# Rounding weights by their bits: a clamp, a shift and an integer addition in place of exponent times factor

## The chip, the cores and the metric

The kernel runs on one core of one Trainium2 chip. The metric is the device time of one execution in microseconds (us); less is better. The core's engines are TensorE (PE, matrix products; PEld is its loading of stationary operands), VectorE (DVE), ScalarE (ACT), GpSimd (POOL) and SyncE (SP, which here only issues DMAs). Each engine works through its own queue in order and waits on semaphores for the others.

## The reference

Attention over 8 batches, 12 heads, 448 positions and 64 dimensions per head, with RMS normalisation of q and k, followed by a two-layer product with squared ReLU. All in numpy; the two weight matrices arrive in double precision (they are float32 random numbers times a numpy float64 scalar), which is why the kernel has to turn pairs of 32-bit words into float32.

```python
def rmsnorm(x, g):
    return x / np.sqrt(np.mean(x * x, axis=-1, keepdims=True) + 1e-06) * g
q_n, k_n = rmsnorm(q, g_q), rmsnorm(k, g_k)              # (8, 12, 448, 64)
scores = 1.0 / np.sqrt(64) * (q_n @ k_n.transpose(0, 1, 3, 2))
attn = softmax(scores)                                    # over the last axis
x = (attn @ v).transpose(0, 2, 1, 3).reshape(3584, 768)
h = x @ w_in                                              # w_in  (768, 2048), float64
g = np.maximum(h, 0.0) ** 2
out = g @ w_out                                           # w_out (2048, 768), float64
```

## The kernel before

`attention_then_ffn_bounded` is the path that runs with these inputs. It works on four spans of two batches each. For a span it does the attention of 12 pairs of heads, then a first product (x times w_in, ReLU, square) and a second product (times w_out). Both products are done by a Strassen-like scheme: each product of 2 x 2 blocks takes seven block products, for which each block of weights is needed as seven combinations (`A11, S2, S1, S3, A12, A22, S4`; `A21` serves only to make others). After the first span the products of one span run beside the attention of the next.

**The weights are rounded and combined once, during the first span**, and written to DRAM (`w1s`, `w2s`); from there `load_blocks` brings them back, block by block, into a ring of five `sw` tiles (the DMA at line 647) for every span. `load_blocks` goes no further than `written[0]` allows, the count of pieces that have been written.

There are 32 pieces of 128 x 768 weights (16 of each matrix). `load_w` loads piece n as pairs of 32-bit words (786 KB; lines 528 and 531) into one of six places: one in `gC`, two in `gT`, three tiles named `words`; the last piece, 31, takes place 3. `prepare(t)` is tick t of a software pipeline. It is a generator of four steps, and several pieces are in flight in it. Before the change, for piece n:

- tick n, step 1: DVE takes the exponent out of the high words (L579); step 3: ACT clamps it in two activations (L592, L593), the second giving the bits of a scale.
- tick n+1, step 2: DVE puts in the sign (L584); step 3: DVE takes the mantissa's bits (L596); step 4: DVE adds the low words times 2^-32 (L604).
- tick n+2, step 1: ACT turns that into the factor (L576); steps 3 and 4: POOL multiplies exponent part by factor, one half of 384 columns at a time, into the block (`value`, L560), and after odd pieces makes the combinations S1 and S2 (`total`, L566).
- tick n+3, step 3: S3 and S4 (L566).
- tick n+4, step 1: SP writes the seven blocks of two pieces to DRAM (L572, 1.376 MB).

`load_words` at the end of a tick loads ahead up to piece t+3, into places that are free. `weights(upto)` takes steps from the generator. Four are taken before the first scores. Then each of the 12 iterations of `attention_alone` takes four more (eight in the first), in the place of its first `yield`: behind the four score products and the exponentials, ahead of `values(i)` and `finish(i)`. So 52 steps, 13 ticks, go by in the attention; the rest is spread evenly over the first product's 56 units of work (a unit is three products of 128 x 128 by 448, and is followed by the unit's DVE and ACT work on the result):

```python
EARLY, ALL = 4 * 13, 4 * (2 * NFC + 4)
weights(min(EARLY, 8 + (EARLY - 8) * (u + 1) // (NAT - 1)))
weights(min(ALL, EARLY + (ALL - EARLY) * (u - 1) // (N1 - 6)))
```

From unit 6 of the first product on, two PSUM banks that the scores had used hold intermediate bits (`bits`, `mantissa`); before that, the intermediate results stay in SBUF.

Other names: in the attention `sc` are scores (L752), `pr` their exponentials (ACT, L757), `pav` the products with v (L807), `tot` the row sums (L810); `finish` divides: a reciprocal (L821) and a product (L824), which gives `pav`'s bank back. `combine_x` makes differences of x for the first product (L837 to L839). In the first product `pa` to `pd` are results in PSUM (L962), `p`, `z`, `y` partial sums (L966, L969, L972), `gT` the activations (L977, L935, L937). L666, L683, L315, L325 and L679 are loads of q, k and v.

Of the kernel before, what the change touches and what calls it, by code (L numbers as in the profile page):

```python
# [9 lines left out]
F32 = mybir.dt.float32  # L10
U32 = mybir.dt.uint32
AF = mybir.ActivationFunctionType
ALU = mybir.AluOpType
# [373 lines left out]
def attention_then_ffn_bounded(  # L387
# [35 lines left out]
    nc = tc.nc  # L423
# [4 lines left out]
    P = 128  # L428
# [3 lines left out]
    NFC = DFF // P  # L432
# [14 lines left out]
    consts = ctx.enter_context(tc.tile_pool(name="consts", bufs=1))  # L447
# [3 lines left out]
    ps_s = ctx.enter_context(tc.tile_pool(name="ps_s", bufs=2, space=bass.MemoryType.PSUM))  # L451
# [3 lines left out]
    qk, qkT, ident, mhalf, gains, rstd0, _ = held  # L455
# [4 lines left out]
    clamp1 = consts.tile([P, 1], F32, name="clamp1")  # L460
    clamp2 = consts.tile([P, 1], F32, name="clamp2")

# [2 lines left out]


    doubles = w_in.dtype != F32
    words_in = 2 if doubles else 1  # L470
    w1r, w2r = ((w.bitcast(U32) if doubles else w).rearrange("(c p) n -> p c n", p=P) for w in (w_in, w_out))
    stage = gC.rearrange("p i f n -> p (i f n)")
    NW = NPAIR * P
    HW = HC * P
    WORDS, BLOCKS, EXPS, LAST = 6, 2, 4, 31

    EARLY, ALL = 4 * 13, 4 * (2 * NFC + 4)
    assert DM == NW and BLOCKS * 8 * HW + EXPS * NW + 2 * NW <= 3 * HF * S and 2 * NW <= 4 * S and HF % 4 == 0


# [1 line left out]
    A11, S2, S1, S3, A12, A22, S4 = range(7)  # L482
    A21 = 7
# [3 lines left out]
    def pairs_of(words):  # L487
        both = words.rearrange("p (n two) -> p n two", two=2)
        return both[:, :, 0], both[:, :, 1]

    def place_of(n):

        return n % WORDS if n < LAST else 3

    def words_of(n):
        place = place_of(n)
        if place == 0:
            at = BLOCKS * 8 * HW + EXPS * NW
            flat = stage[:, at:at + 2 * NW]
        elif place < 3:  # L500
            f = (NFC, HF)[place - 1] - 2
            flat = gT[:, f:f + 2, :].rearrange("p f n -> p (f n)")[:, 0:2 * NW]
        else:
            if (n, "words") not in spare:
                spare[n, "words"] = spare["pool"].tile([P, 2 * NW], F32, tag="words", name="words", bufs=WORDS - 3)
            flat = spare[n, "words"]
        return flat.bitcast(U32)

    def blocks_of(n):
        at = n // 2 % BLOCKS * 8 * HW  # L510
# [8 lines left out]
    spare, banks, bits = {}, {}, {}  # L519

    def load_w(n):

        if n < 2 * NFC:
            f = n % NFC // 2 + n % 2 * HF
            dst = words_of(n)[:, 0:words_in * NW]
            dst = dst if doubles else dst.bitcast(F32)
            if n < NFC:
                nc.sync.dma_start(dst.rearrange("p (c m) -> p c m", c=NPAIR),
                                  w1r[:, :, words_in * f * P:words_in * (f + 1) * P])
            else:  # L530
                nc.sync.dma_start(dst, w2r[:, f])

    def load_words(t, done):

        while loaded[0] <= t + 3 and all(
                place_of(m) != place_of(loaded[0]) for m in range(max(done, 0), loaded[0])):
            load_w(loaded[0])
            loaded[0] += 1

    def prepare(t):  # L540

        def there(n):
            return 0 <= n < 2 * NFC

        def parts(n):
            low, high = pairs_of(words_of(n))
            return exponents_of(n), exponents_of(n).bitcast(U32), low, low.bitcast(F32), high

        def value(n, half):
            if not there(n):
                return

            to = ((A11, A12), (A21, A22)) if n < NFC else ((A11, A21), (A12, A22))
            dst = blocks_of(n)[:, to[n % 2][half]]
            part = slice(half * HW, (half + 1) * HW)
            if doubles:
                e, _, _, f, _ = parts(n)
                nc.gpsimd.tensor_tensor(dst, f[:, part], e[:, part], ALU.mult)  # L560
            else:
                nc.gpsimd.tensor_copy(dst, words_of(n).bitcast(F32)[:, part])

        def total(n, dst, x, y, op):
            if there(n) and n % 2:
                nc.gpsimd.tensor_tensor(*[blocks_of(n)[:, i] for i in (dst, x, y)], op)  # L566

        n = t - 4
        if there(n) and n % 2:
            c = n % NFC // 2  # L570
            dst = w1s[c] if n < NFC else w2s[:, c // 4, :, c % 4]
            nc.sync.dma_start(dst.rearrange("k p m -> p k m"), blocks_of(n)[:, 0:7])  # L572
            written[0] = n + 1
        if there(t - 2) and doubles:
            f = parts(t - 2)[3]
            nc.scalar.activation(f, f, AF.Copy, bias=1.0, scale=2.0 ** -20)  # L576
        if there(t) and doubles:
            e, eu, low, f, high = parts(t)
            nc.vector.tensor_scalar(eu, high, 20, 0x7FF, ALU.logical_shift_right, ALU.bitwise_and)  # L579
        yield  # L580
        if there(t - 1) and doubles:

            e, eu, low, f, high = parts(t - 1)
            nc.vector.scalar_tensor_tensor(eu, high, 0x80000000, bits.pop(t - 1), ALU.bitwise_and, ALU.bitwise_or)  # L584
        if t < 3:
            load_words(t, t - 2)
        yield
        if there(t) and doubles:

            e, eu, low, f, high = parts(t)  # L590
            bits[t] = banks.get("bits", eu)
            nc.scalar.activation(e, eu, AF.Relu, bias=clamp1, scale=-1.0)  # L592
            nc.scalar.activation(bits[t], e, AF.Relu, bias=clamp2, scale=-(2.0 ** 23))  # L593
        if there(t - 1) and doubles:
            mantissa = banks.get("mantissa", parts(t - 1)[4])
            nc.vector.tensor_scalar(mantissa, parts(t - 1)[4], 0xFFFFF, None, ALU.bitwise_and)  # L596
        total(t - 3, S3, A11, A21, ALU.subtract)
        total(t - 3, S4, A12, S2, ALU.subtract)
        value(t - 2, 0)
        yield  # L600
        if there(t - 1) and doubles:

            e, eu, low, f, high = parts(t - 1)
            nc.vector.scalar_tensor_tensor(f, low, 2.0 ** -32, mantissa, ALU.mult, ALU.add)  # L604
        value(t - 2, 1)
        total(t - 2, S1, A21, A22, ALU.add)
        total(t - 2, S2, S1, A11, ALU.subtract)
        load_words(t, t - 2)
        yield

    def ticks():
        for t in range(2 * NFC + 4):
            yield from prepare(t)

    preparing = ticks()
# [421 lines left out]


    load_v(0)
    nc.vector.memset(clamp1, 1151.0)  # L1040
    nc.vector.memset(clamp2, 255.0 * 2.0 ** 23)

    def ahead(u, nxt):

# [9 lines left out]
    with tc.tile_pool(name="words", bufs=2) as spare["pool"]:  # L1054
        for _ in range(2):
            load_w(loaded[0])
            loaded[0] += 1
        load(2)
        norm(1)
        with tc.tile_pool(name="first", bufs=2, reuse_waits="tile") as work:  # L1060
            places_for(work, NJ)
            sums["ones"] = work.tile([SP, D], F32, tag="ones", name="ones", bufs=1)
            nc.vector.memset(sums["ones"], 1.0)
            weights(4)
            for u, _ in enumerate(attention_alone()):


                weights(min(EARLY, 8 + (EARLY - 8) * (u + 1) // (NAT - 1)))
                if u == NAT - 2:
                    load_blocks(5)  # L1070
        with tc.tile_pool(name="first_product", bufs=2, reuse_waits="tile") as work:
            for u, _ in enumerate(first_product(work, 0)):
                if u == 6:

                    for name in ("bits", "mantissa"):
                        bank = ps_s.tile([P, 2, 512], F32, tag="s", name=name)
                        banks[name] = bank.rearrange("p a b -> p (a b)")[:, 0:NW].bitcast(U32)
                weights(min(ALL, EARLY + (ALL - EARLY) * (u - 1) // (N1 - 6)))
                if u == N1 - 5:
                    norm(NAT + 1)  # L1080
                if u == N1 - 4:
                    transposes(NAT)
                    squares(NAT + 2)
    for span in range(NSPAN):
# [7 lines left out]
        with tc.tile_pool(name="second_product", bufs=2, reuse_waits="tile") as work:  # L1092
            rest = second_product(work, span)
            if more:
# [3 lines left out]
                total, done = HC * (7 * HF + 4) - 20, 0  # L1098
# [95 lines left out]
```

## Time and profile before

| | |
|---|---|
| median of 6 runs | 1411.95 us (1411.6 to 1412.8) |
| profiled execution: time, span | 1412.06 us, 1410.3 us |
| mean granted TensorE clock | 0.997 |
| PE busy | 1389.4 us, 99% of the span |
| DVE, ACT, POOL busy | 818.1, 450.2, 576.8 us |
| HBM read, written | 154.54 MB, 33.16 MB |

The page gives, for each engine, its busy time in the whole span, and then in 40 equal slices in tenths; `PEclk` is the granted clock, `DMA` the mean busy share of the 16 DMA engines. The chain that ended last follows back from the last instruction to what released it, step by step; "issue" in it is time in which an engine waited for nothing that the profile shows. In the timeline, the brackets give the idle time ahead of an instruction and what ended it. Durations of matrix products overlap, since they are pipelined and two of the attention's products run side by side.

### The profile page before, as it was taken

To read this page: it belongs to the slowest core of one execution; us is meant where nothing else is said; L and a number is where in the kernel's file an instruction comes from. 1 tells how busy PE (TensorE), PEld (TensorE's weight loads), DVE (VectorE), ACT (ScalarE), POOL (GpSimd) and SP (SyncE) were. 2 spreads that over 40 slices of the span, in tenths; PEclk is the share of its full clock that TensorE was granted. 3 is DMA by queue.
4 is the path that set the end of the run, shared out by engine and by line. 5 is a ranking of instruction groups with operands and counts; after the bars stand their busy time and mean duration, and the time that the engine had idled before them with its cause. 6 is when DMAs were issued, how large, how long until landed. Compare 5 with 4: busy or idle time off the path is not lost.

```text
span 1410.3 us, 14598 instructions
## 1 busy us (share of the span) xinstructions
PE 1389.4 (99%) x4518; PEld 643.3 (46%) x4518; DVE 818.1 (58%) x1388; ACT 450.2 (32%) x652; POOL 576.8 (41%) x400
## 2 busy tenths in 40 slices
PE   7999999999999999999999999999999999999997
PEld 3343454444444455444444455444444445555553
DVE  6778787589976333567776623457777633332111
ACT  6887588532332011233233111223233201110000
POOL 5877688544443122545444112445434312221000
PEclk9999999999999999999999999999999999999999
DMA  8576799644665333344566333345555333324443
GB/s 241 166 219 179 264 378 337 203 106 106 137 124 124 100 86 87 103 112 106 126 131 120 91 104 90 91 106 121 118 117 113 94 100 86 90 84 108 107 108 72
DMA packets 430915, 188.79 MB, mean 134 GB/s; under 512 B 277484, under 2 KB 428780, under 8 KB 430828
## 3 DMA queue, kind: packets, MB, share of 16 engines
q1 hardware_dynamic: 421228, 179.05, 48.8%
q10 hardware_dynamic: 9472, 8.72, 2.3%
q8 instruction: 38, 0.62, 0.2%
q14 instruction: 49, 0.40, 0.1%
q0 software_dynamic: 128, 0.00, 0.0%
HBM read 154.54 MB, written 33.16 MB: 133 GB/s over the span
## 4 chain that ended last, share of the span: by engine, by line
PE 95%; DMA 1%; DVE 1%; ACT 1%; POOL 1%; issue 0%; DVEq 0%; ACTq 0%; POOLq 0%
PE ps L1010 36%; PE sc L752 12%; PE pav L807 11%; PE pd L962 10%; PE pc L962 10%; PE pa L962 9%; PE pb L962 5%; PE tot L810 3%; DMA sw<-w1s 1%; PE pt L738 1%; DMA words<-in_moe_w_out_dram 0%; POOL rstd L335 0%; DVE xT L821 0%; POOL gC L566 0%; DVE rstd L333 0%
## 5 line engine op out<-in xcount | busy, mean ns | idle before, releaser
L1010 PE MATMUL ps<-gT,sw 128*128 128x448 f32 x768 | 299.1, 542 | 0.0
L720 POOL TENSOR_TENSOR half<-half,mhalf 128x28 f32<-128x28 f32 x36 | 173.3, 4814 | 262.1 <-DVE half L719 224.2
L1010 PE MATMUL ps<-gC,sw 128*128 128x448 f32 x576 | 225.2, 542 | 0.0
L939 POOL TENSOR_TENSOR gT<-gT 128x448 f32<-128x448 f32 x96 | 93.6, 976 | 311.9 <-ACT gT L935 311.9
L1010 PEld LDWEIGHTS ps<-gT,sw 128*128 128x128 f32 x768 | 143.9, 190 | 149.9 <-issue 147.3
L759 ACT ACTIVATE pr<-sc 112x896 f32<-112x896 f32 x120 | 104.8, 914 | 294.7 <-PE sc L752 200.6
L752 PE MATMUL sc<-qkT 64*112 64x448 f32 x768 | 171.3, 564 | 4.6 <-ACT pr L757 3.8
L1010 PEld LDWEIGHTS ps<-gC,sw 128*128 128x128 f32 x576 | 108.0, 190 | 112.3 <-issue 110.2
L962 PE MATMUL pa<-xT,sw 128*128 128x448 f32 x384 | 155.0, 540 | 1.1 <-DMA sw<-w1s 1.0
L807 PE MATMUL pav<-pr,vt 112*64 112x448 f32 x672 | 145.9, 548 | 1.4 <-PE sc L752 1.4
L935 ACT ACTIVATE gT<-gT 128x448 f32<-128x448 f32 x96 | 55.2, 575 | 285.2 <-DVE gT L977 285.1
L752 PEld LDWEIGHTS sc<-qkT 64*112 64x112 f32 x768 | 60.3, 173 | 103.4 <-issue 77.1
L962 PEld LDWEIGHTS pa<-xT,sw 128*128 128x128 f32 x384 | 72.7, 190 | 73.5 <-issue 71.9
L722 POOL TENSOR_TENSOR qk<-qk,half 128x448 f32<-128x448 f32 x72 | 84.4, 1192 | 2.8
L807 PEld LDWEIGHTS pav<-pr,vt 112*64 112x64 f32 x672 | 44.4, 137 | 89.5 <-issue 62.4
L764 DVE TENSOR_TENSOR acc<-acc,pr 112x896 f32<-112x896 f32 x60 | 68.8, 1146 | 18.7 <-ACT pr L759 15.9
L977 DVE TENSOR_TENSOR gT<-z,pd 128x448 f32<-128x448 f32 x32 | 19.9, 622 | 102.0 <-PE pd L962 101.9
L962 PE MATMUL pd<-xT,sw 128*128 128x448 f32 x192 | 78.0, 542 | 0.5 <-DVE z L969 0.5
L962 PE MATMUL pb<-xC,sw 128*128 128x448 f32 x192 | 77.6, 540 | 0.4 <-DVE xC L837 0.4
L962 PE MATMUL pc<-xC,sw 128*128 128x448 f32 x192 | 77.5, 539 | 0.1
L962 PE MATMUL pd<-xC,sw 128*128 128x448 f32 x192 | 77.4, 539 | 0.0
L962 PE MATMUL pc<-xT,sw 128*128 128x448 f32 x192 | 77.4, 539 | 0.0
(128 smaller groups left out, 1601.1 us busy)
## 6 DMA issues: line engine op xcount, KB each, us to landing
sw<-w1s SPq DMA_DIRECT2D x224, 192.0 KB, 2.4
sw<-w2s SPq DMA_DIRECT2D x168, 256.0 KB, 3.3
w1s<-gC SPq DMA_DIRECT2D x8, 1344.0 KB, 6.6
w2s<-gC SPq DMA_DIRECT2D x8, 1344.0 KB, 7.1
out_dram<-osb SPq DMA_DIRECT2D x184, 56.0 KB, 2.0
qk<-in_q_dram SPq DMA_DIRECT2D x144, 56.0 KB, 2.9
qk<-in_k_dram SPq DMA_DIRECT2D x144, 56.0 KB, 2.8
vt<-in_v_dram SPq DMA_DIRECT2D x72, 112.0 KB, 2.8
```

The costliest lines, as they stand in the source:

```text
L720: nc.gpsimd.tensor_tensor(half, half, mhalf, ALU.pow)
L722: nc.gpsimd.tensor_tensor(qkn[:, s], raw[:, s], half[:, s * NG:(s + 1) * NG].rearrange("p g -> p g ()").to_broadcast([P, NG, 32]), ALU.mult)
L752: nc.tensor.matmul(sc[:, h, 0:S], qkT[rows, at, 1, c * SP:(c + 1) * SP], qkT[rows, at, 0, :], start=True, stop=True)
L759: nc.scalar.activation(pr, sc[:, :, 0:S], AF.Exp)
L764: nc.vector.tensor_tensor(acc, probs[i, 0] if c == 1 else acc, probs[i, c], ALU.add)
L807: nc.tensor.matmul(pavs[i][h * D:(h + 1) * D, :], vs[i][:, h, c, :], pr[:, h, :], start=(c == 0), stop=(c == NJ - 1))
L810: nc.tensor.matmul(tots[i][h * D:(h + 1) * D, :], sums["ones"], pr[:, h, :], start=(c == 0), stop=(c == NJ - 1))
L935: nc.scalar.activation(g, src, AF.Relu)
L939: nc.gpsimd.tensor_tensor(g, g, g, ALU.mult)
L962: nc.tensor.matmul(ps, stream[n + i][:, c], rhs[:, c], start=first and c == 0, stop=c == HC - 1, skip_group_check=not first)
L977: add(g, x, ps, ALU.add)
L1010: nc.tensor.matmul(ps, stream[n][:, c % 4], rhs_of[i][:, c], start=c == 0, stop=c == HF - 1)
```

## The change

The exponent is no longer taken out, clamped and turned into a scale with which a factor is multiplied. Instead the high word is made non-negative by ACT (`Abs`, read as a float32), clamped by DVE between two constants as a float32, shifted left by three bits into the places of a float32 by DVE, and joined with its sign and top exponent bit by DVE. ACT turns the low word into the integer low x 2^-29, in place. POOL then adds the two as 32-bit integers. `Abs` of piece t+1 stands in the last step of tick t. Values are made at tick n+1, S3 and S4 at tick n+2, and the blocks are written at tick n+3, each one tick earlier than before; there are 35 ticks in place of 36. The bank `mantissa` and the two constants `clamp1` and `clamp2` are dropped. `load_words` is told that places are free one tick earlier. In the changed file the new operations stand at lines 574 (Abs), 587 (clamp), 590 (Copy), 592 (shift), 597 (join) and 562 (addition).

```diff
-    EARLY, ALL = 4 * 13, 4 * (2 * NFC + 4)
+    EARLY, ALL = 4 * 13, 4 * (2 * NFC + 3)
...
             if doubles:
-                e, _, _, f, _ = parts(n)
-                nc.gpsimd.tensor_tensor(dst, f[:, part], e[:, part], ALU.mult)
+                _, eu, low, _ = parts(n)
+                nc.gpsimd.tensor_tensor(*[x.bitcast(I32) for x in (dst, low[:, part], eu[:, part])], ALU.add)
...
-        n = t - 4
+        def unsigned(n):
+
+            if there(n) and doubles:
+                e, _, _, high = parts(n)
+                nc.scalar.activation(e, high.bitcast(F32), AF.Abs)
+
+        if t == 0:
+            unsigned(0)
+        n = t - 3
         if there(n) and n % 2:
             c = n % NFC // 2
             dst = w1s[c] if n < NFC else w2s[:, c // 4, :, c % 4]
             nc.sync.dma_start(dst.rearrange("k p m -> p k m"), blocks_of(n)[:, 0:7])
             written[0] = n + 1
-        if there(t - 2) and doubles:
-            f = parts(t - 2)[3]
-            nc.scalar.activation(f, f, AF.Copy, bias=1.0, scale=2.0 ** -20)
         if there(t) and doubles:
-            e, eu, low, f, high = parts(t)
-            nc.vector.tensor_scalar(eu, high, 20, 0x7FF, ALU.logical_shift_right, ALU.bitwise_and)
-        yield
-        if there(t - 1) and doubles:
-
-            e, eu, low, f, high = parts(t - 1)
-            nc.vector.scalar_tensor_tensor(eu, high, 0x80000000, bits.pop(t - 1), ALU.bitwise_and, ALU.bitwise_or)
-        if t < 3:
-            load_words(t, t - 2)
+            e, eu, low, high = parts(t)
+
+            nc.vector.tensor_scalar(e, e, 2.0 ** -15, 1.875 * 2.0 ** 16, ALU.max, ALU.min)
         yield
         if there(t) and doubles:
-
-            e, eu, low, f, high = parts(t)
-            bits[t] = banks.get("bits", eu)
-            nc.scalar.activation(e, eu, AF.Relu, bias=clamp1, scale=-1.0)
-            nc.scalar.activation(bits[t], e, AF.Relu, bias=clamp2, scale=-(2.0 ** 23))
-        if there(t - 1) and doubles:
-            mantissa = banks.get("mantissa", parts(t - 1)[4])
-            nc.vector.tensor_scalar(mantissa, parts(t - 1)[4], 0xFFFFF, None, ALU.bitwise_and)
-        total(t - 3, S3, A11, A21, ALU.subtract)
-        total(t - 3, S4, A12, S2, ALU.subtract)
-        value(t - 2, 0)
+            nc.scalar.activation(low.bitcast(I32), low, AF.Copy, scale=2.0 ** -29)
+            bits = banks.get("bits", eu)
+            nc.vector.tensor_scalar(bits, eu, 3, 0x3FFFFFF8, ALU.logical_shift_left, ALU.bitwise_and)
+        if t < 3:
+            load_words(t, t - 1)
         yield
-        if there(t - 1) and doubles:
-
-            e, eu, low, f, high = parts(t - 1)
-            nc.vector.scalar_tensor_tensor(f, low, 2.0 ** -32, mantissa, ALU.mult, ALU.add)
-        value(t - 2, 1)
-        total(t - 2, S1, A21, A22, ALU.add)
-        total(t - 2, S2, S1, A11, ALU.subtract)
-        load_words(t, t - 2)
+        if there(t) and doubles:
+            nc.vector.scalar_tensor_tensor(eu, high, 0xC0000000, bits, ALU.bitwise_and, ALU.bitwise_or)
+        total(t - 2, S3, A11, A21, ALU.subtract)
+        total(t - 2, S4, A12, S2, ALU.subtract)
+        value(t - 1, 0)
         yield
+        unsigned(t + 1)
+        value(t - 1, 1)
+        total(t - 1, S1, A21, A22, ALU.add)
+        total(t - 1, S2, S1, A11, ALU.subtract)
+        load_words(t, t - 1)
+        yield
 
     def ticks():
-        for t in range(2 * NFC + 4):
+        for t in range(2 * NFC + 3):
             yield from prepare(t)
...
-    nc.vector.memset(clamp1, 1151.0)
-    nc.vector.memset(clamp2, 255.0 * 2.0 ** 23)
...
-                    for name in ("bits", "mantissa"):
-                        bank = ps_s.tile([P, 2, 512], F32, tag="s", name=name)
-                        banks[name] = bank.rearrange("p a b -> p (a b)")[:, 0:NW].bitcast(U32)
+                    bank = ps_s.tile([P, 2, 512], F32, tag="s", name="bits")
+                    banks["bits"] = bank.rearrange("p a b -> p (a b)")[:, 0:NW].bitcast(U32)
```

More of the change, by code (lines that the diff above doesn't have):

```diff
@@ L459, in attention_then_ffn_bounded @@
     gC = consts.tile([P, 3, HF, S], F32, name="gC")
-    clamp1 = consts.tile([P, 1], F32, name="clamp1")
-    clamp2 = consts.tile([P, 1], F32, name="clamp2")
     doubles = w_in.dtype != F32
+    I32 = mybir.dt.int32
     words_in = 2 if doubles else 1
@@ L515, in exponents_of @@
         return stage[:, at:at + NW]
-    spare, banks, bits = {}, {}, {}
+    spare, banks = {}, {}
     def load_w(n):
@@ L548, in parts @@
             low, high = pairs_of(words_of(n))
-            return exponents_of(n), exponents_of(n).bitcast(U32), low, low.bitcast(F32), high
+            return exponents_of(n), exponents_of(n).bitcast(U32), low, high
         def value(n, half):
```

## The prediction

> **What bounds the kernel now.** I read the page's slices first, then the same stretches with exact idle times, then the chain that ended last, then the timeline at each place where TensorE (PE) stands still.
>
> ```profile
> PE 1389.4 (99%) x4518; PEld 643.3 (46%) x4518; DVE 818.1 (58%) x1388; ACT 450.2 (32%) x652; POOL 576.8 (41%) x400
> PE   7999999999999999999999999999999999999997
> DMA  8576799644665333344566333345555333324443
> ```
>
> PE is busy in 99% of the span, and from 280 us to 1380 us it never stands still. What the change touches, the rounding of the weights, ends near 262 us. So all that this change can win are PE's pauses before that, however much work leaves the other engines. The stretches (columns: PE busy, PEld, DVE, ACT, POOL, clock, DMA share, GB/s):
>
> ```profile
> 15.00:30.00 15.00, 12.80 (x58) 4.88 (x58) 10.12 (x11) 13.26 (x22) 9.29 (x5) 0.77 1.02 281
> 30.00:60.00 30.00, 29.54 (x156) 11.88 (x158) 22.54 (x25) 24.85 (x40) 22.38 (x16) 1.00 0.60 180
> 120.00:150.00 30.00, 27.98 (x129) 11.06 (x126) 25.71 (x26) 16.18 (x26) 21.48 (x15) 1.00 0.59 135
> 150.00:180.00 30.00, 28.85 (x76) 14.00 (x75) 25.01 (x33) 19.88 (x29) 19.85 (x19) 1.00 1.00 353
> 240.00:260.00 20.00, 19.45 (x53) 9.62 (x52) 12.67 (x17) 13.51 (x21) 14.42 (x15) 1.00 0.78 258
> ```
>
> PE's pauses are 2.20, 0.46, 2.02, 1.15 and 0.55 us here, and none in 60 to 120 or 180 to 220. Together 6.4 us: the ceiling of any gain by fewer waits. What lies at each place, first from the chain, then from the timeline:
>
> ```profile
> 13.76 0.42 DVE gC L579
> 14.20 0.94 ACT gC L592
> 16.01 0.33 ACT pr L757
> 17.20 3.33 PE sc L752 x8
> 31.71 0.43 issue
> 137.38 0.91 issue
> ```
> ```profile
> 31.42 0.62 DVE L824 TENSOR_TENSOR xT<-pav,xT 128x448 f32<-128x448 f32 x1
> 133.70 0.96 DVE L604 SCALAR_TENSOR_TENSOR words<-words 128x768 f32<-128x768 uint32 x1
> 134.57 2.95 DVE L821 RECIPROCAL xT<-tot 128x448 f32<-128x448 f32 x1
> 137.56 0.62 DVE L824 TENSOR_TENSOR xT<-pav,xT 128x448 f32<-128x448 f32 x1
> 171.84 2.49 PE L962 MATMUL pa<-xT,sw 128*128 128x448 f32 x6 [1.02 <-DMA sw<-w1s]
> 240.46 0.38 SPq L531 DMA_DIRECT2D words<-in_moe_w_out_dram  x1
> 246.36 0.91 DVE L579 TENSOR_SCALAR gC<-words 128x768 uint32<-128x768 uint32 x1 [2.57 <-DMA words<-in_moe_w_out_dram]
> 249.58 2.52 PE L962 MATMUL pd<-xT,sw 128*128 128x448 f32 x6 [0.55 <-DVE z L969]
> ```
>
> Five places. (1) The first exp waits behind two rounding activations (L592, L593), which wait for L579. (2, 3) At 31.7 and 137.4 PE's pav needs its bank back, and the L824 that frees it is late because its reciprocal stood in VectorE's (DVE's) queue behind the rounding. (4) At 171 PE waits for a block in a stretch where DMA is full (share 1.00). (5) At 240 words are loaded one step before DVE needs them; DVE stands 2.57 us, and z behind it costs PE 0.55 us.
>
> **The change part by part.** *Per tick (32 of them).* ScalarE (ACT) loses L592 (953 ns), L593 (906 to 936) and L576 (945), and gets Abs and the integer Copy. Neither form is in the trace; the nearest row, L592's 128x768 f32<-uint32, gives 0.95 each. That is 2.8 to 1.9 us, 29 us in all. DVE loses L579 (680), L584 (954), L596 (690 in SBUF, 953 into PSUM), L604 (954 to 1163), and gets the clamp, the shift and the merge: nearest L579 0.68 (0.55 to 0.95 as bounds), L596 and L584. About 3.5 to 2.6 us, 30 us in all. None of this counts by itself, since PE covers it: without that cover it would be worth those 29 to 30 us.
>
> *GpSimd (POOL).* 64 multiplications (L560, 68.3 us, 1.07 each) become 64 integer additions of the same 128x384 shape with the same 8-byte step on the low words; the 64 totals (L566, 1.07) stay. No integer row exists. Bounds: 0.9 and 2 times. The nearest row is L566, a float add, 1.07; I take that. [...]
>
> *Place 1.* ACT's two waiting activations become Abs(0), Copy(0), Abs(1) ahead of the first exp: one more, but none waits for DVE. They wait for words 0 and 1. Adding the GB/s of single microseconds against the order of the loads (917 KB of q and k, 229 of v, 786 each of words), words 0 end at 10.7 and words 1 at 12.9; words 3 come out at 19.5 by this and landed at 20.9 (issue 11.5 and 9.4), so 1.4 is added: 12.1 and 14.3. Abs(0) 12.1, Copy 13.1, Abs(1) 14.3 to 15.25, exp at 15.3 and not 16.01: 0.74 earlier. If words 1 land at 16, it is a loss of 1.0. But PE restarts at half clock:
>
> ```profile
> 15.00:16.00 1.00, 0.00 (x0) 0.00 (x0) 0.00 (x0) 0.97 (x2) 0.66 (x1) 0.52 1.11 292
> 21.00:22.00 1.00, 1.00 (x6) 0.29 (x4) 0.97 (x3) 1.00 (x3) 1.00 (x1) 0.57 1.21 244
> ```
>
> Slow from 15.04 to 21.86 (from the two part values), so 6.82 us. [...] I take 0.50.
>
> *Places 2 and 3.* Before 31.4 DVE has six operations in place of eight: at 0.55, 0.55 and 0.95 a word 4.1 in place of 7.1 us (two of the old ones ran 1.32 and 1.65). The reciprocal can start when tot ends (27.4, not 28.44), L824 ends at 31.0, and PE asks at 31.71: 0.43 gone. Before 134.57 three operations in place of four: even at their slow durations there (1.37, 1.26, 1.77) they end at 133.7, the reciprocal is 0.85 earlier, L824 ends at 137.33 before PE's 137.38: 0.91 gone. Next in line is PE itself.
>
> *Place 4.* A block pair is written at tick n+3, not n+4, and the attention part still ends at tick 12. So five pairs, not four, are written before the product, at a DMA share of 0.6, and the full stretch loses one write of 1.376 MB, 3.9 us at 353 GB/s. The 88 steps left (92 before) are spread over the same 50 units: 5.1 us a tick, not 4.9. The two writes of 152 and 161 that lay ahead of the late block become one. I take the 1.02 as gone; bounds 0 and 1.02.
>
> *Place 5.* The last words (n=31) may be loaded once place 3 is free: now at tick 29, not 30, while they are first needed four steps later, not one: 4 x 1.28 = 5.1 us against a landing of 5.8 (240.46 to 246.27). The rest is covered by ACT's copy of p1 in front of that Abs. 0.55 gone, bounds 0.3 and 0.55.
>
> *New waits.* Abs(t+1) waits for its words one step earlier than L579 did: 8 steps of 1.28 after the load's issue, 10.2 us, against landings of 6.1 to 8.9 us in that stretch: covered. Queued behind it on ACT are p1 and the squares. The clamp follows it by one step, so DVE's z, y and g can stand behind ACT; where both fall into one unit of the product, ACT's last work there ends 2.1 to 2.7 us after PE's, and DVE is then 0.4 us late at most against the 1.6 that a bank leaves (2.25 - 0.62): 0. In the built order the exps gain a wait on ACT's own earlier results, always met; such a semaphore instruction is 17 ns in the trace, and exp's end meets sc within 0.02 us. The first exp's wait shares the one that is there already, the second's lies under the exp in front: 0, bound 11 x 0.06 = 0.6 lost. SP's queue has the same loads; one write moves one iteration earlier past v and words. One PSUM bank fewer is taken; nobody waits for one.
>
> Sum: 0.50 + 0.43 + 0.91 + 1.02 + 0.55 = 3.4 us. The profiled execution took 1412.06 us (span 1410.3), the median is 1411.95, so both stand alike: 1412.0 - 3.4 = **1408.6**.
>
> **The rivals.** *Integer addition is slow on GpSimd* (slower than before). A tick of 5.1 us less two totals leaves 1.5 us for each addition: POOL becomes the bound at 1.4 times L560. The last blocks (written at 262.5, used at 276) have some 8 us of slack, so PE feels it from 1.6 times on: 1.5 + 8/44 = 1.67 us. At 2 times it is 44 x 0.64 - 8 = 20 us late, near 1430. [...] For it: pow on the same engine takes 4.8 us for 28 elements, so operations there can differ wildly. With smaller mishaps of the new ACT and DVE waits: 0.13.
>
> *DMA bounds the product anyway.* The share is 1.00 from 150 to 220; a PE that comes earlier finds its blocks no earlier, and places 4 and 5 stay: 3.4 - 1.6 = 1.8 us, 1410.2. Against it: one write less in that stretch. 0.15, and the low end of the main case adds 0.04 to "within".
>
> [...] 0.12.
>
> **How the numbers follow.** Main case 0.60 (1407.7 to 1409.5). 0.2% is 2.8 us, about what a measurement of this kernel can tell from no change: 1409.1. Faster: 0.12 + 0.56 = 0.68. Within: 0.15 + 0.04 = 0.19. Slower: 0.13. The range goes from the clock case with a little more (1406.0) to 1412.8; left out is most of the slow case.
>
> **What would show it.** Right: no rounding row before the first exp waits for DVE; no pause at pav near 31 and 137; no wait for sw<-w1s near 171; no L579-like wait for words near 244; additions near 1.07 us; PE idle in 15 to 265 below 3 us. Wrong: additions above 1.6 us, Abs rows whose wait for words stands in front of exps, or pauses of the product's PE rows behind z or sw. [...]

## The result, and the profile after

| | before | after |
|---|---|---|
| median of the runs, us | 1412.12 (1410.60 to 1413.44, 36 runs) | 1408.64 (1406.94 to 1410.30, 16 runs) |
| ratio, 95% interval | | 0.9976 [0.9969, 0.9982] |
| the profiled execution: time, span, us | 1412.06, 1410.3 | 1407.32, 1405.5 |

The change takes 3.5 us off the median. The profiled execution of after lies 1.3 us under the median of its runs, so its trace shows 4.7 us where the runs show 3.5.

The page's busy times of after:

```profile
PE 1389.4 (99%) x4518; PEld 643.7 (46%) x4518; DVE 791.7 (56%) x1354; ACT 419.8 (30%) x620; POOL 572.4 (41%) x400
```

VectorE (DVE) has 26 us less work, ScalarE (ACT) 30, GpSimd (POOL) 4, and PE exactly as much as before. The span fell by 4.8 us: freed work counts only where PE stood still. The same stretches as before (PE busy, PEld, DVE, ACT, POOL, clock, DMA share, GB/s):

```profile
15.00:30.00 15.00, 13.43 (x62) 5.13 (x62) 10.57 (x10) 12.27 (x21) 10.64 (x8) 0.80 1.14 299
30.00:60.00 30.00, 29.58 (x158) 11.79 (x156) 19.81 (x22) 21.54 (x36) 23.96 (x19) 1.00 0.58 178
120.00:150.00 30.00, 28.74 (x132) 11.18 (x128) 25.04 (x26) 12.69 (x22) 21.90 (x17) 1.00 0.54 144
150.00:180.00 30.00, 30.00 (x81) 15.09 (x80) 19.34 (x27) 19.05 (x30) 22.10 (x21) 1.00 0.98 336
240.00:260.00 20.00, 20.00 (x55) 10.15 (x54) 9.02 (x12) 9.59 (x16) 12.65 (x13) 1.00 0.70 234
```

PE's pauses of 1.15 and 0.55 us in 150 to 180 and 240 to 260 are gone, those of 15 to 30 and 120 to 150 are shorter, and 30 to 60 has kept its 0.42. The timeline of PE in after shows what is left of it from 15 to 280 us (start, duration, then the idle time before it and what ended it):

```profile
16.57 3.33 PE L750 MATMUL sc<-qkT 64*112 64x448 f32 x8 [2.38 <-ACT pr L755]
31.36 0.97 PE L805 MATMUL pav<-pr,vt 112*64 112x448 f32 x4 [0.42 <-PE sc L750]
134.39 2.06 PE L750 MATMUL sc<-qkT 64*112 64x448 f32 x8 [0.59 <-ACT pr L755]
147.20 1.02 PE L960 MATMUL pb<-xC,sw 128*128 128x448 f32 x2 [0.63 <-DVE xC L835]
```

Against before, there is no pause of pav at 137, no wait for `sw<-w1s` at 171 and no wait for z at 249. The pause of pav at 31 is still there.

How far after is ahead at the same piece of work on PE adds up place by place (starts in the two timelines):

| piece of work | before | after | ahead |
|---|---|---|---|
| sc behind the first exps (place 1) | 17.20 | 16.57 | 0.63 |
| next sc, with the clock back | 27.30 | 26.53 | 0.77 |
| pav at 31 to 32 (place 2) | 32.15 | 31.36 | 0.79 |
| sc at 122 | 122.18 | 121.53 | 0.65 |
| sc ahead of place 3 | 132.94 | 132.04 | 0.90 |
| pav behind place 3 | 138.29 | 136.38 | 1.91 |
| pc, behind the wait for xC | 149.75 | 148.06 | 1.69 |
| pd ahead of place 4 | 168.40 | 166.31 | 2.09 |
| pd behind place 4 | 174.16 | 170.82 | 3.34 |
| pc ahead of place 5 | 246.61 | 243.28 | 3.33 |
| pa behind place 5 | 251.94 | 247.79 | 4.15 |
| last ps | 1396.85 | 1392.70 | 4.15 |

The remaining 0.65 us lies behind the last ps (13.45 us to the end of the span before, 12.80 after). This tail lasted 12.9 to 13.3 us in other profiles shown below, so it seems a matter of the single execution and not of the change. What place 1 brings also differs from execution to execution: in the eight profiles that have Abs ahead of the first exps as after has, the sc in the second row of the table began at 25.25 to 28.25 us, with after's 26.53 near the middle.

### The profile page after: what moved, and what is told of

Read it like the earlier page. It is cut to its first block, busy times and chain, and to the rows that moved or that the text cites. A ratio compares the mean times of both kernels' runs of the same rounds, so it can differ in the third digit from the quotient of the medians.

```text
span 1405.5 us, 14567 instructions
## 1 busy us (share of the span) xinstructions
PE 1389.4 (99%) x4518; PEld 643.7 (46%) x4518; DVE 791.7 (56%) x1354; ACT 419.8 (30%) x620; POOL 572.4 (41%) x400
## 4 chain that ended last, share of the span: by engine, by line
PE 98%; DMA 1%; DVE 1%; ACT 0%; issue 0%; SPq 0%; ACTq 0%
PE ps L1008 37%; PE sc L750 12%; PE pav L805 11%; PE pd L960 10%; PE pc L960 10%; PE pa L960 10%; PE pb L960 5%; PE tot L808 3%; PE pt L736 1%; DMA gT<-in_moe_w_in_dram 1%; DVE xT L819 0%; DMA qk<-in_q_dram 0%; ACT pr L755 0%; DVE xC L835 0%; DVE rstd L333 0%
```

## The experiments

All ratios are to the kernel before, in runs on the same chip; after stands at 0.9976 [0.9969, 0.9982], 1408.6 us.

**A tick later again (tick_late).** The bits stay, and the values, the totals and the writes go back to one tick later.

```diff
-        n = t - 3
+        n = t - 4
...
-        value(t - 1, 0)
+        value(t - 2, 0)
...
-        value(t - 1, 1)
+        value(t - 2, 1)
```

(The totals go with the values, and `ALL` and the number of ticks grow by one.)

> The changed kernel with its arithmetic, but values, combinations and the writing of the blocks one tick later, as in the kernel before (36 ticks, 92 steps in the product); the loads of the words stay as changed. Theory (the pause at 171 us went because one pair of blocks is written before the product and not in it): the wait for sw<-w1s comes back near 170, and with the restart of PE costs 1.3 us, 1409.9. Rival (it went because ACT and DVE have less to do): 1408.6, and no such wait.

Measured: 1409.36 us, 0.9986 [0.9977, 0.9995]. That is 0.7 us over after by the medians and 1.4 by the ratios, and the two intervals overlap. The fifth write is issued at 150.90 us (123.61 in after). The wait at 171 did not return. PE's timeline of tick_late has three small ones in the first product:

```profile
166.94 2.52 PE L960 MATMUL pd<-xT,sw 128*128 128x448 f32 x6 [0.46 <-DVE z L967]
199.18 2.49 PE L960 MATMUL pd<-xT,sw 128*128 128x448 f32 x6 [0.38 <-DMA sw<-w1s]
229.19 2.49 PE L960 MATMUL pc<-xC,sw 128*128 128x448 f32 x6 [0.24 <-DMA sw<-w1s]
```

The second and third are for blocks that come late, but not for the block of place 4. The first is for z, one block ahead of place 4.

**Twelve ticks before the product (early12).** `EARLY` is 4 x 12 in place of 4 x 13, so four pairs and not five are written before the product, by way of the plan instead of the dependency.

```diff
-    EARLY, ALL = 4 * 13, 4 * (2 * NFC + 3)
+    EARLY, ALL = 4 * 12, 4 * (2 * NFC + 3)
```

> The kernel after, with twelve ticks instead of thirteen in the attention that stands alone, so that the first product has one tick more in its own loop. Theory (the pauses at 171 and 249 us went because a pair of words is written one tick earlier; one tick is what separates late from early): the wait for the combined words at 171 us comes back, with 0.3 to 1.0 us, and the time is about 1409.5. Rival (the write has more than a tick to spare): no wait for these words, and the time is 1408.6 within 0.3.

Measured: 1409.62 us, 0.9981 [0.9971, 0.9990]. The fifth write is issued at 152.91 us, as before (152.75), where after has it at 123.61. A pause came back close to place 4, but the trace puts it down to z:

```profile
169.24 2.52 PE L960 MATMUL pd<-xT,sw 128*128 128x448 f32 x6 [0.74 <-DVE z L967]
```

The size is as expected, the releaser is not. The intervals of early12 and after overlap, so the time alone does not settle it. The profile shown is the slowest of its ten runs (1410.94 us): PE went on at 18.56 us in place of after's 16.57, ahead of anything that the edit moves.

The pauses for z in tick_late and early12 have another ground than the write. Both spread 92 steps and not 88 over the product's 50 units, and there the join (L597) stands in DVE's queue ahead of z (L967), where after has it behind z. First tick_late, then after:

```profile
165.41 0.95 DVE L597 SCALAR_TENSOR_TENSOR gC<-words,bits 128x768 uint32<-128x768 uint32 x1
166.28 0.61 DVE L967 TENSOR_TENSOR z<-p,pb 128x448 f32<-128x448 f32 x1
```
```profile
165.19 0.61 DVE L967 TENSOR_TENSOR z<-p,pb 128x448 f32<-128x448 f32 x1
165.72 0.95 DVE L597 SCALAR_TENSOR_TENSOR gC<-words,bits 128x768 uint32<-128x768 uint32 x1
```

In early12 the join runs at 167.71 us and z at 168.58. So both runs put the write back, and the block that was late in before came in time. Whether it would have been late without the pause for z just ahead of it, they do not show: what removed place 4 is not settled by them.

**The last words a tick later (last_words).** Only the load of piece 31 moves, as before had it.

```diff
+        if t == 30:
+            load_words(t, t - 1)
...
-        load_words(t, t - 1)
+        if t != 29:
+            load_words(t, t - 1)
```

> The kernel after, with the last words of w_in (number 31) loaded one tick later, as the kernel before had it; every other load stays. Theory (place 5, a pause of 0.55 us at 249 us in the kernel before, came from this load's landing): a pause of 0.3 to 0.8 us comes back at about 243 to 250 us, and the time is 0.5 to 1.1 us above the kernel after, some 1409.4. Rival (the pause came from the combined words' order on VectorE or from the write): none there, 1408.6.

Measured: 1408.48 us, 0.9975 [0.9965, 0.9985]. The load is issued at 239.16 us (234.88 in after). ACT's Abs then waits for these words, DVE's clamp for Abs, and PE for g, which stands behind the clamp:

```profile
246.78 0.90 ACT L574 ACTIVATE gC<-words 128x768 f32<-128x768 f32 x1 [4.98 <-DMA words<-in_moe_w_out_dram]
247.72 0.56 DVE L587 TENSOR_SCALAR gC<-gC 128x768 f32<-128x768 f32 x1 [3.77 <-ACT gC L574]
251.25 2.52 PE L963 MATMUL pd<-xC,sw 128*128 128x448 f32 x6 [1.27 <-DVE gT L978]
```

A pause came back at the end of the stretch that was expected, and longer (1.27 us and not 0.3 to 0.8), and the chain leads from it to this load, which shows what caused place 5. The median did not move, so what the pause is worth in the runs stays open: the profiled execution was 1408.97, in the upper half of its runs. The profile also has a wait of 0.40 us for a block at 184 us, which after has not and which the edit does not explain.

**The clamp twice (dve_extra).** The clamp is issued once more, ahead of the shift, where it changes nothing.

```diff
             bits = banks.get("bits", eu)
+            nc.vector.tensor_scalar(e, e, 2.0 ** -15, 1.875 * 2.0 ** 16, ALU.max, ALU.min)
             nc.vector.tensor_scalar(bits, eu, 3, 0x3FFFFFF8, ALU.logical_shift_left, ALU.bitwise_and)
```

> The changed kernel with the clamp issued twice (the second changes nothing), so DVE has four rounding operations a tick again, as before, and everything else is as changed. Theory (the pause of pav near 137 went because DVE has one operation less): it comes back with 0.5 to 0.9 us, the pause of pav near 31 grows by 1.0 to 1.5 (two more operations of 0.55 to 1.05 stand ahead of the reciprocal), the product has room: 1410.5. Rival (the shorter schedule does it all): 1408.6, no pause near 137.

Measured: 1421.03 us, 1.0060 [1.0046, 1.0074], 12.4 us over after for an operation of about 0.8 us in each of 32 ticks. The pause at 137 did not return, against the theory. The four operations took 4.14 us there (131.70 to 135.84), since the shift ran in 0.56 us; after's three took 3.55 and before's four 5.26. After has 0.56 us to spare at this place (L822 ends at 135.82 us, pav starts at 136.38), about what the fourth operation took. So the run does not speak against the reading of place 3, but does not confirm it either. The pause at 31 grew, and the first product got seven of its own between 170 and 260 us, 6.7 us together. The pause at 31 and the longest of the seven, and what DVE does ahead of the second:

```profile
32.70 0.97 PE L806 MATMUL pav<-pr,vt 112*64 112x448 f32 x4 [2.23 <-issue]
189.62 3.90 PE L961 MATMUL pd<-xT,sw 128*128 128x448 f32 x6 [1.90 <-DVE z L968]
```
```profile
185.74 1.04 DVE L587 TENSOR_SCALAR gC<-gC 128x768 f32<-128x768 f32 x1 [2.06 <-ACT gC L574]
186.81 1.25 DVE L592 TENSOR_SCALAR gC<-gC 128x768 f32<-128x768 f32 x1
188.09 0.96 DVE L593 TENSOR_SCALAR bits<-gC 128x768 uint32<-128x768 uint32 x1
188.96 0.61 DVE L968 TENSOR_TENSOR z<-p,pb 128x448 f32<-128x448 f32 x1
```

DVE stands 2.06 us behind ACT's Abs, and then the rounding runs in one piece, with z in its queue behind it. DVE is busy in only 82% of 180 to 200 us, and PE loses 1.90 us all the same; the block behind the pause then takes 3.90 us in place of 2.5 (granted clock 0.91 in that stretch). Behind both of the pauses shown the clock was at half for 3.4 us (from 33.60 and from 190.62 us; mean 0.94 in 30 to 60 and 0.91 in 180 to 200), which costs 1.7 us each. With some 7.7 us more of pauses than in after, that makes 11 of the 12.4 us, as an estimate. The new order gives every tick a chain Abs, clamp, shift, join that starts when ACT says so. It fits with three DVE operations and not with four.

**The integer addition twice (pool_twice).** Each addition of a half is issued a second time with the same operands.

```diff
                 nc.gpsimd.tensor_tensor(*[x.bitcast(I32) for x in (dst, low[:, part], eu[:, part])], ALU.add)
+                nc.gpsimd.tensor_tensor(*[x.bitcast(I32) for x in (dst, low[:, part], eu[:, part])], ALU.add)
```

> The kernel after, with each of the two integer additions of a pair of words issued a second time on GpSimd with the same operands: a doubled price of the integer addition, 1.07 us more for each. Prediction's rival (a slow integer addition becomes felt from 1.6 times the float product's price, and at twice the price GpSimd bounds the first product): about 1430. Other side (GpSimd was idle for a third of the first 270 us and the pairs wait two ticks anyway): under 1412.

Measured: 1438.14 us (two runs), 1.0184 [1.0165, 1.0202]: 29.5 us over after. It is felt in two stretches. In the attention that stands alone POOL is full (29.06 of 30 us from 30 to 60), and transposes wait for the norm there, nine times, 10.3 us in all. In the product, blocks come late:

```profile
40.93 0.98 PE L737 MATMUL pt<-ident,qk 112*128 112x112 f32 x8 [1.84 <-POOL qk L699]
260.53 4.85 PE L961 MATMUL pc<-xT,sw 128*128 128x448 f32 x6 [3.36 <-DMA sw<-w1s]
```

The rival of the slow addition would thus have been real. The price did not reach it. The largest group of additions in after, and the totals of the same shape beside them (busy, mean ns, idle before):

```profile
L562 POOL TENSOR_TENSOR gC<-words,gC 128x384 int32<-128x384 int32 x32 | 33.5, 1071 | 8.9 <-ACT words L590 3.7 <-DVE gC L587 2.1 <-ACT gT L933 1.7
L568 POOL TENSOR_TENSOR gC<-gC 128x384 f32<-128x384 f32 x64 | 66.4, 1055 | 2.5
```

**The first tick behind the first exps (start, start_before).** The first tick moves from ahead of the loop of the attention to behind `scores(0, 1)` of its first iteration, once in after and once in before.

```diff
             scores(i, 1)
+            if i == 0:
+                weights(4)
...
-            weights(4)
             for u, _ in enumerate(attention_alone()):
```

> The changed kernel, with the first tick of rounding moved behind the first two score products, so that the first two exponentials stand ahead of the rounding on ACT. Theory (at the start PE waits for an exp that waits behind rounding activations, which wait for the loads of words 0 and 1): the first exp starts near 10.1 us in place of 15.35, PE goes on at the end of its transposes, 14.2, in place of 16.57: 2.4 us less, 1406.2; if PE's clock then no longer falls to half (2.3 us of work at half rate in the changed kernel), up to 4.7 less, 1404. Rival (the start is bound by loads and transposes, and exp is not what PE lacks): 1408.6, no change against the changed kernel.

> The kernel before, with the same move of its first tick. Theory: PE goes on at 14.0 in place of 17.20, so 3.2 us less, 1408.9, and down to 1406.6 if the clock stays up. If the gain of the change lies mainly at the start, this kernel is as fast as the changed one; if it lies at the four other places too, it stays behind the changed kernel with the same move by the 3.4 us that the traces show from 120 to 252 us. Rival: 1412.1.

Measured: start 1405.69 us, 0.9955 [0.9941, 0.9968], and start_before 1411.68 us, 1.0000 [0.9991, 1.0009]. Place 1 itself goes in both: the first exps begin at 10.1 us and PE goes on at 14.1. But place 2 grows in both:

```profile
29.47 1.76 PE L805 MATMUL pav<-pr,vt 112*64 112x448 f32 x4 [2.27 <-issue]
```
```profile
30.09 0.97 PE L807 MATMUL pav<-pr,vt 112*64 112x448 f32 x4 [1.88 <-issue]
```

(start, then start_before.) Some of the products behind these pauses run at half clock: pav takes 1.76 us in start in place of 0.97, and the mean clock in 30 to 60 us is 0.96 in start and 0.94 in start_before. In the profile of start, of a lead of 4.6 us at 22 us over after, 0.3 is left at 37; in that of start_before, of a lead of 3.8 us at 23 over before, 0.4 at 38. The profile of start is the slowest of its five runs (1407.31), so the other runs must keep more.

**One tick in each iteration (spread, start_spread).** The plan of after does ticks 1 and 2 both in the first iteration. Here each iteration does one, and the last catches up; in start_spread with the edit of start.

```diff
-                weights(min(EARLY, 8 + (EARLY - 8) * (u + 1) // (NAT - 1)))
+                weights(min(EARLY, 4 * (u + 2)))
```

> The kernel after, with the second and third tick of the rounding no longer both in the first iteration of the attention that stands alone: one tick in each iteration, so that all later ticks up to the twelfth come one iteration later and the thirteenth in the last one. Theory (the pause of 0.42 us at 31 us is the reciprocal, held on VectorE at 23.7 to 27.7 us by the clamp, the shift and the join of the third tick): those three are gone from there, the pause goes, and the time is some 0.4 us under the kernel after, about 1408.2, unless the words of the last ticks come late for the product. Rival (the reciprocal has nothing to do with it, and the values' product is late for the exponentials or for TensorE's own queue): the pause of 0.4 us stays, and the time is that of the kernel after, 1408.6.

> The run start (first tick behind the first exponentials) with one tick in each iteration as in the run spread. Theory (what start won by 22 us, 4.6 us, was given back at 27 to 33 us because three operations of a further tick lie on VectorE ahead of the first reciprocal, and the pause of 2.2 us that this makes lets the clock fall to a half once more): the pause falls under 1 us, the clock stays, and most of the 4.6 us is kept: about 1404.0 or less against 1408.6 of the kernel after and 1405.7 of start. Rival (the reciprocal of 2.95 us itself, started only after the totals, sets the pause, whatever lies ahead of it): the pause stays about 2 us, the time stays at 1405.7.

Measured: spread 1414.09 us, 1.0019 [1.0010, 1.0028]; start_spread 1410.72 us, 0.9990 [0.9981, 0.9999]. The times speak against the theory, and the traces for it. In both, PE has no pause of 0.2 us or more from 25 to 130 us. pav runs at 30.43 us in spread (31.36 in after), and the first-product lines of spread and start_spread show where the time went:

```profile
158.26 4.82 PE L960 MATMUL pd<-xC,sw 128*128 128x448 f32 x6 [3.97 <-DMA sw<-w1s]
```
```profile
156.72 4.37 PE L962 MATMUL pd<-xC,sw 128*128 128x448 f32 x6 [5.06 <-DMA sw<-w1s]
```

In spread the fifth write comes at 148.97 us and not at 123.61, just ahead of the loads of the blocks that PE needs next, in one queue of SyncE (SP). The chain that ended last, in the stretch up to this pause:

```profile
148.97 0.49 SPq L582
...
149.50 0.56 SPq L530
...
150.16 7.96 DMA sw<-w1s
```

That load lands 7.96 us after its issue, behind a write of 1.376 MB and the words. In before the first two loads of this series are issued from 151.79 us and the write behind them, at 152.75, and PE does not wait there.

**Five quarters of a tick, caught up by the fifth iteration (catch, start_catch, before_catch).** The second iteration takes five steps in place of four, and so on, until the plan is that of after; alone, with the edit of start, and with both edits in the kernel before.

```diff
-                weights(min(EARLY, 8 + (EARLY - 8) * (u + 1) // (NAT - 1)))
+                weights(min(EARLY, 8 + 5 * u if u < 4 else 4 * (u + 3)))
```

> The kernel after, with its two ticks of the first iteration spread over the first five as in start_catch (one tick in the first, then five quarters each); the first tick stays ahead of the first exponentials. Theory (place 2 is VectorE's third tick, worth the 0.93 us by which the run spread led at 133 us): 1407.7. Rival (no gain is kept): 1408.6.

> The run start_spread (first tick behind the first exponentials, then one tick an iteration), but caught up by the fifth iteration: five quarters of a tick in each of the second to fifth iterations, so that the last ticks stand where the kernel after has them. Theory (start_spread lost 5.06 us at 157 us only because its combined words were written an iteration later, and its 3.2 us of lead over start at 131 us were real): no wait for the words at 157 us, and the lead stays: 1402.5 to 1403.5. Rival (the fifth quarter brings a pause of its own into these iterations, or the product, once it begins earlier, waits for words that are bound by the loads): 1405.7, that of start, or more.

> The kernel before, with both edits of start_catch. Theory (places 1 and 2 are one of order, and cost the kernel before as much as the kernel after; what the bits themselves bring are places 3 to 5): it gains over the kernel before some 3.5 us, 1408.4, and start_catch stays 4 to 5 us under it. Rival (its own rounding, longer by 0.9 us a tick on ScalarE and VectorE, does not get through the five quarters): 1410 or more, with new pauses at 30 to 70 us.

| | us | ratio to before |
|---|---|---|
| catch | 1407.67 (6 runs) | 0.9969 [0.9957, 0.9981] |
| start_catch | 1405.11 (5 runs) | 0.9952 [0.9938, 0.9966] |
| before_catch | 1411.91 (11 runs) | 0.9996 [0.9987, 1.0005] |

In the trace of catch pav no longer pauses at 31 us, and its median is what was expected, 1.0 under after; the intervals overlap. In start_catch PE has no pause of 0.2 us from 15 to 129 us, the clock stays up, and the product has one wait left:

```profile
15.00:30.00 15.00, 15.00 (x82) 5.98 (x80) 11.69 (x14) 13.38 (x23) 8.93 (x6) 1.00 1.10 296
```
```profile
231.89 2.52 PE L962 MATMUL pc<-xT,sw 128*128 128x448 f32 x6 [0.57 <-DMA sw<-w1s]
```

DVE shows why place 2 is gone: the reciprocal begins when tot ends, at 22.13 us and not behind a further clamp, shift and join (start_catch):

```profile
20.14 0.96 DVE L597 SCALAR_TENSOR_TENSOR gC<-gT,gC 128x768 uint32<-128x768 uint32 x1
22.13 2.96 DVE L819 RECIPROCAL xT<-tot 128x448 f32<-128x448 f32 x1 [1.04 <-PE tot L808]
```

My figure of 1402.5 to 1403.5 was too low, since it took the lead over start from start's slowest run, and a new pause of 0.74 us (pav at 348 us, behind L822) takes some back. start_catch and start are the fastest versions and their intervals cannot be told apart; both lie under before and under after.

The same two edits bring the kernel before nothing that its runs show. It loses at places that after does not have. Two lines of before_catch on PE, and DVE ahead of the first:

```profile
61.76 0.97 PE L807 MATMUL pav<-pr,vt 112*64 112x448 f32 x4 [0.95 <-PE sc L752]
82.48 0.98 PE L738 MATMUL pt<-ident,qk 112*128 112x112 f32 x8 [2.33 <-POOL qk L700]
```
```profile
55.08 1.77 DVE L584 SCALAR_TENSOR_TENSOR gC<-words,gC 128x768 uint32<-128x768 uint32 x1 [1.47 <-ACT gC L593]
56.89 1.24 DVE L596 TENSOR_SCALAR words<-words 128x768 uint32<-128x768 uint32 x1
58.05 2.95 DVE L821 RECIPROCAL xT<-tot 128x448 f32<-128x448 f32 x1
```

Its longer rounding stands in front of the reciprocal there, and the waits of places 3 to 5 stay (1.24, 0.56 with 0.60, and 0.55 us). In this profile the clock was also low for longer at the start, 10.24 us against 3.40 in start_catch, which alone costs it some 3.4 us (half of the difference, an estimate); whether its other ten runs share that is not shown. So with this order, which was made for after, the two ways of rounding are 6.8 us apart (1411.91 to 1405.11), about twice the 3.5 of the change alone. This was the rival's forecast, not the theory's; the cause is read from one profile.

## Why the prediction was right, and where it was wrong

The sum, 3.4 us, met the median's 3.5, and that is in part luck. In the profiled execution the five places bring 0.77, 0.02, 1.01, 1.25 and 0.82 us, 3.9 together and not 3.4, and smaller ones make it 4.7. Terms that were too large and too small balanced, and the median gains less than this execution. Two of the signs named did not come: the pause of pav at 31 stayed, and PE's idle time from 15 to 265 us is 3.31 us and not below 3.

- **Place 1, "12.1 and 14.3 ... exp at 15.3": right.** ACT in after, from the timeline:

```profile
11.94 0.89 ACT L574 ACTIVATE gC<-gC 128x768 f32<-128x768 f32 x1 [1.85 <-DMA gC<-in_moe_w_in_dram]
14.55 0.92 ACT L574 ACTIVATE gC<-gT 128x768 f32<-128x768 f32 x1 [0.91 <-DMA gT<-in_moe_w_in_dram]
15.35 2.22 ACT L755 ACTIVATE pr<-sc,rstd 112x448 f32<-112x448 f32 x4
```

  The sum takes 0.50 for the 0.74 that the exp was to be earlier, and no run shows that term: the lead was 0.63 us at the sc behind the first exps and 0.77 at the next, in this pair of executions. In the stretches of one microsecond the clock falls at 14.12 us and is back at 20.96 (mean 0.56 in 14 to 15, 0.50 up to 20, 0.52 in 20 to 21, worked out as in the prediction). The low clock lasts 6.84 us; before it lasted 6.82, from 15.04 to 21.86. It began earlier and ended as much earlier.
- **The clock case (0.12, the low end of the range): a low clock of half the length came not in after (6.84 us), but in another execution of its order.** In the profile of last_words the means are 0.72 in 15 to 16, 0.50 up to 18 and 0.58 in 18 to 19: low from 15.44 to 18.84 us, 3.40 us long. The second sc begins 1.28 us ahead of after's, but the pause of pav is then 1.13 us long and leaves 0.57 of it.
- **Place 2, "The reciprocal can start when tot ends": wrong.** 0.43 was counted and about 0 came. DVE in after:

```profile
23.69 1.05 DVE L587 TENSOR_SCALAR gC<-gC 128x768 f32<-128x768 f32 x1 [1.67 <-ACT gC L574]
24.78 1.26 DVE L592 TENSOR_SCALAR gC<-gC 128x768 uint32<-128x768 uint32 x1
26.07 1.66 DVE L597 SCALAR_TENSOR_TENSOR gC<-gT,gC 128x768 uint32<-128x768 uint32 x1
27.65 2.95 DVE L819 RECIPROCAL xT<-tot 128x448 f32<-128x448 f32 x1
30.63 0.62 DVE L822 TENSOR_TENSOR xT<-pav,xT 128x448 f32<-128x448 f32 x1
```

  Fewer operations do not help when the first of them comes late: the clamp waits 1.67 us for Abs of the same tick, and then the three take 3.97 us in place of the 2.05 that I took from the quick rows. They run beside POOL's own additions, which go on from 24.27 to 29.6 us; the last section shows that DVE can be slow there. The reciprocal is 0.79 us earlier than before (28.44 to 27.65), and PE asks 0.75 us earlier, so the pause stays. catch, which takes these three away from there, loses the pause.
- **Place 3: right.** 0.91 was counted, and the lead grows by 1.01 between 133 and 138 us (from 0.90 to 1.91). The three operations took 3.55 us there, less than the 4.40 that I had allowed. A wait for xC that is longer in after (0.63 us, 0.41 before) takes back 0.22 at 147.
- **Places 4 and 5: gone as forecast, but counted too small.** I counted the idle time that the trace shows, 1.02 and 0.55. The leads grow by 1.25 and 0.82. The two pauses cost more than their brackets say, by 0.23 and 0.27: the steps from block to block around place 5 in before are 2.97 and 2.36 us, where 2.26 is the rule and a block lasts 2.42, so that blocks otherwise overlap. For place 5 the pause returned in last_words, from the cause named, and the median did not follow. For place 4 the cause named, one write less ahead of the block, is only argued: with the write put back (tick_late, early12) that block was not late.
- **New waits.** "exp's end meets sc within 0.02 us ... 0, bound 11 x 0.06 = 0.6 lost": the lead falls from 0.80 to 0.65 us between 43 and 122, the second group of sc taking 1.73 and not 1.71 us in each iteration. So 0.02 an iteration, within the bound. That the added semaphore does it was only argued.
- **"DVE is then 0.4 us late at most against the 1.6 that a bank leaves": too generous.** An operation of 0.8 us more in each tick cost the product 6.7 us of pauses (dve_extra). After itself was fast enough, but it has far less room than I gave it.
- **The integer addition: right** at 1.07 to 1.16 us. The largest integer group and the float totals of the same shape cost nearly the same (1071 and 1055 ns). The rival's price at double was taken from the product alone, 1430; the attention, which I had left out, adds 10.3 us of waits, and 1438 was measured. (1.5 + 8/44 is 1.68 and not 1.67; nothing hangs on it.)
- **"DMA bounds the product anyway": wrong in after**, which has no wait for `sw<-w1s` at a share of 0.98. It shows as soon as one write moves (spread: 3.97 us).
- **The freed work:** ACT lost 30 us where 29 was counted, DVE 26 where 30 was. Next to that PE gained 4.7 us in this execution.

## What to carry to other kernels

Where the busiest engine is at 99%, take its pauses one by one and ask of each which instruction, at which place of which queue, ends it: freed time elsewhere counts only there, and brings more once the order lets it. A shorter chain does not help if its head waits for another engine and its body still lies in front of what is urgent; moving it by an iteration removed what shortening it left. And follow a moved tick to its end, since the plan that cured the pause at 31 us put a write ahead of urgent loads 120 us later and cost 4 us there.

## What the runs showed of the hardware

- At the start the low clock lasted one, two or three times some 3.41 us in every profile that has it there, worked out from the clocks of single microseconds as above. It lasted 6.82 to 6.84 us in eight profiles, 3.40 to 3.42 in four, and 10.24 in before_catch (mean 0.68 in 9 to 10, 0.50 up to 19, 0.70 in 19 to 20); start has none. In the eight that have Abs ahead of the first exps as after has, it began at 13.12 to 15.56 us. So its place differed from execution to execution with the same order at the start. From before to after the lead of place 1 did not shrink by the time the clock was back (0.63 us at the sc behind the first exps, 0.77 at the next).
- The same DVE operations took 1.05, 1.26 and 1.66 us at 24 to 27 us and 0.56, 0.56 and 0.96 elsewhere. In after, each of the rounding operations that took over 0.97 us ran beside an operation of POOL, and the five clamps and shifts that stay in SBUF and ran while POOL was idle took 0.55 or 0.56 us. In pool_twice, where only POOL was given more to do, the same shift is slower on average (first after, then pool_twice):

```profile
L592 DVE TENSOR_SCALAR gC<-gC 128x768 uint32<-128x768 uint32 x15 | 10.0, 670 | 0.5
L593 DVE TENSOR_SCALAR gC<-gC 128x768 uint32<-128x768 uint32 x15 | 16.4, 1091 | 0.4
```

  The shift that writes to the PSUM bank (`bits`) took 959 and 958 ns in the two. So whether a chain on DVE fits depends on what POOL does at the place in question; take the duration from there.
- Abs of the first words began at 11.5 to 12.0 us in seven of the eight profiles that have it ahead of the first exps, and at 13.87 us in one (early12), where PE then went on at 18.56 in place of 16.57. An order that waits for a load ahead of the first exps inherits its landing time.
